# Second pass of the first MoE in chunk pairs: 512 moving columns per weight, one routing per pair

## The chip, the cores and the metric

The kernel runs on one core of a Trainium2 chip. The metric is the device time of one launch in microseconds, as the median of several runs. One of the executions is taken by the hardware profiler; every row below is from that one. PE is TensorE (PEld its weight loads), DVE is VectorE, ACT is ScalarE, POOL is GpSimd, SP is SyncE, which issues most DMAs.

## What is computed

Three stages in a row, cut here to what matters:

```python
attn = softmax(window-128 scores with ALiBi) @ v      # (4, 8, 576, 64)
x = attn as (2304, 512)
h = x @ w_in                                          # (2304, 2048)
x = softplus(h) @ w_out                               # the first MoE, (2304, 512)
logits = x @ w_gate + log1p(exp(x @ w_noise)) * noise # 8 experts
top2 of each token, softmax over the two
out[t] = sum over its two experts of weight * (relu(x[t] @ w1[e]) @ w2[e])
```

## The kernel before, in words

The 2304 tokens go through the first MoE in nine chunks of 256 (`CT`), and the 2048 hidden features in 16 slices of 128 (`NF`). All of a slice of `w_in` and `w_out` is held as a high and a low float32r part. One **unit** is one chunk times one slice: `mm1` (line 574) multiplies the slice of `w_in` with the chunk through `up` (line 539), which is 12 matmuls of 256 moving columns (four pieces of the contraction, three products high-high, high-low, low-high each), into one PSUM bank `h`; then a chain of small operations makes the softplus and splits it into `gh` and `gl` (lines 597 to 606: Abs, Exp and Ln on ACT; `u` and the first sum on DVE; two sums in halves on POOL through `by_halves`, line 570; the cast `gh` and the rest `gl` on DVE); then `mm2` (line 615) multiplies `gh` and `gl` with the slice of `w_out` through `down` (line 563), six matmuls of 512 columns, into the two accumulators of the chunk.

The units stand in the list `jobs` (line 1405). The first pass takes the slices 0 to 5 (`NA`) of all chunks while the attention still runs, and stores partial sums in DRAM. The second pass takes the slices 6 to 15 of chunk 0, then of chunk 1, and so on: 90 units. In the main loop (line 1459) unit t's `mm1` is followed by `mm2` of unit t-3, with `side_work` (line 1425) after each of the two: it takes one step from the list of the routing. `x_load` (line 642) brings a chunk's input back from DRAM for the second pass, `part_load` its partial sum, `y_evac` (line 670) adds the two on DVE and stores the result to `x1buf`.

`route` (line 809) then gives the steps of the router for that chunk: two `r_transpose` (four PE transposes each, ACT copies the result), `r_logits`, `r_sum`, `r_top2` (some 25 small DVE operations), `r_rank` (positions of the tokens in each expert's list, five small matmuls and DVE steps), and then four indirect DMAs on POOL that scatter the records (`rect<-rec,pi`, line 803). `early_table` (line 971) makes from the counts of chunks 0 to 5 the first four groups of the second MoE; their weights (`raw`), record lists (`rk`) and rows (`xg`) are then loaded. In the last seven units of the pass `w2_split` (line 1215) already splits weights of the second MoE, ACT the high part `whi` and DVE the low part `wlo`. The second MoE follows, with `up_wide` (line 555), which already uses 512 columns.

Every engine carries its instructions out in the order in which they were written. That order comes from a planner with modelled costs (`Order`, line 24): a chain's next step is written when the model says that it is due. `tl` gives out tiles in rings: the third tile of a ring of two waits for the first one's last reader.

Of the kernel before, what the change touches and what calls it, by code (L numbers as in the profile page):

```python
# [18 lines left out]
P = 128  # L19
# [91 lines left out]
def moe_chain_kernel(ctx, tc, qk, v, w_in, w_out, w_gate, w_noise, noise, w1, w2, out):  # L111
# [14 lines left out]
    NLEAD = 3  # L126

# [158 lines left out]
    def xt_tile(c):  # L286
        if c not in XT:
            if c == 2:
                XT[c] = tuple(wpool.tile([P, KC, CT], F32R, name=n, tag="w", bufs=NRING) for n in ("xh2", "xl2")) + (None,)
            else:  # L290
                XT[c] = x_tile(2, ("mm1", c))
# [259 lines left out]
    def x_tile(bufs, fin):  # L551
        x2 = tl(mid, [P, 2, KC, CT], F32R, "xhl", bufs, fin)
        return x2[:, 0], x2[:, 1], x2

# [19 lines left out]
    def mm1(t):  # L574
# [10 lines left out]
        if fc == NA:  # L585
            for z in range(2):
                need(("xi", c, z))
            if c + 1 < NCH:
                x_load(c + 1)
        w = W[2 * fc]  # L590
        ph = up(lambda z, kc: w[:, z, kc * P:(kc + 1) * P], XT[c], CT, ("hr", t))
# [23 lines left out]
    def mm2(t):  # L615
        c, fc = divmod(t, NF)
        if c == 0:
            weights(2 * fc + 1)
        need(("g", t))
        gh, gl = G.pop(t)  # L620
        if fc in (0, NA):
            side_by_side = c == 1 and fc == 0
            if side_by_side:
# [18 lines left out]
    def x_load(c):  # L642
        XT[c] = x_tile(2, ("mm1b", c))
        for z, x in enumerate(XT[c][:2]):
            dma(lambda z=z, x=x: SP.dma_start(f32(x).rearrange("p k t -> p (k t)"), xspill[c, z]),
                ("xi", c, z), 1 << 19)
# [17 lines left out]
    def part_load(c):  # L664
        def load():
            x1, flat = x1_tile(c, ("x1", c))
            SP.dma_start(flat, yspill[c])
        dma(load, ("yi", c), 1 << 19)

    def y_evac(c):  # L670
        need(("yi", c))
        x1 = X1[c]
        for a in range(TT):
            chain(("V", cv(512), lambda a=a: DVE.tensor_add(x1[:, a], Y[c][a], x1[:, a]), ("y%d" % a, c)))
        dma(lambda: SP.dma_start(x1buf[c * CT:(c + 1) * CT, :].rearrange("(a p) n -> p a n", p=P), x1),
            ("x1d", c), 1 << 19, 0.7, (("y0", c), ("y1", c)))


    RT = {}

    def r_transpose(c, tt):
        need(("y0", c))
        need(("y1", c))
        pt = ps_t(("x1T", c, tt)).rearrange("p (c t) -> p c t", c=KC)
        for kc in range(KC):
            tr(pt[:, kc, :], X1[c][:, tt, kc * P:(kc + 1) * P], ident)
        if tt == 0:
            RT[c] = tl(mid, [P, KC, CT], F32, "x1T", 1, ("lgm", c))
        else:
            chain((None, 0, None, ("x1", c), (("x1d", c),)))  # L690
        x1T = RT[c][:, :, tt * P:(tt + 1) * P]
        chain(("A", ca(512), lambda: ACT.activation(x1T, pt, AF.Copy), ("x1T", c, tt)))

    def r_logits(c):

        for tt in range(TT):
            need(("x1T", c, tt))
        pl = ps_t(("lgp", c))[:, :CT]
        for kc in range(KC):
            PE.matmul(pl[32 * kc:32 * kc + 32, :], wgn[:, kc, :], RT[c][:, kc, :], start=True, stop=True)  # L700
        spend(4 * CT / 2.4 + 100)
        mark(("lgm", c))
        lgp = RT[c] = tl(mid, [P, CT], F32, "lgp", 1, ("lgs", c))
        chain(("A", ca(CT), lambda: ACT.activation(lgp, pl, AF.Copy), ("lgp", c)))

    def r_sum(c):
        need(("lgp", c))
        pt = ps_t(("lg", c))[:, :CT].rearrange("p (t k) -> p t k", t=TT)
        for tt in range(TT):
            tr(pt[:, tt], RT[c][:, tt * P:(tt + 1) * P], ident)  # L710
        mark(("lgs", c))
        lg = RT[c] = tl(mid, [P, TT, 2 * E], F32, "lg", 1, ("top", c))
        chain(("V", cv(CT), lambda: DVE.tensor_reduce(
# [4 lines left out]
    def small(name, shape, dtype=F32):  # L718
        return mid.tile(shape, dtype, name="r_" + name, tag="r_" + name, bufs=1)

    def r_top2(c):
        lg = RT[c]
        z = lg[:, :, E:]
# [7 lines left out]
        rec = mid.tile([P, TT, 2, 2], I32, name="rec", tag="rec", bufs=2)  # L731
# [11 lines left out]
        step(DVE.tensor_mul, l, l, nz[:, c * TT:(c + 1) * TT, :])  # L743
# [14 lines left out]
        for k2 in range(2):  # L758
            step(DVE.tensor_copy, rec[:, :, k2, 0], tok[:, c * TT:(c + 1) * TT])
# [11 lines left out]
    def r_rank(c):  # L771
        need(("mb", c))
        r = RT[c]
        pr = ps_t(("rk", c))[:, :TT * E].rearrange("p (a e) -> p a e", a=TT)
        if c:
            need(("mc", c - 1))
# [7 lines left out]
        pi = mid.tile([P, 2, TT], I32, name="pi", tag="pi", bufs=2)  # L784
# [16 lines left out]
        for tt in range(TT):  # L801
            for k2 in range(2):
                G_ += [("P", 1.05, lambda tt=tt, k2=k2: POOL.indirect_dma_start(
                    out=rect[2 * tt + k2], out_offset=bass.IndirectOffsetOnAxis(ap=pi[:, k2, tt:tt + 1], axis=0),
# [4 lines left out]
    def route(c):  # L809
        for _ in range(3):  # L810
            yield None
        yield lambda: r_transpose(c, 0)
        yield lambda: r_transpose(c, 1)
# [8 lines left out]
        for _ in range(6 + 2 * (c == NCH - 2) + 3 * (c == NCH - 1)):  # L822
            yield None
# [45 lines left out]
    p2 = None  # L869
# [4 lines left out]
    def open_p2():  # L874
# [4 lines left out]
        p2 = ctx.enter_context(tc.tile_pool(name="p2", bufs=2))  # L879
        for name, n, base, step in (("jm", 2 * NJ, 0, P // 2), ("jpair", NJ // 2, P, 2 * P), ("jfull", NJ // 2, 2 * P, 2 * P),  # L880
# [231 lines left out]
    def g_gather(g):  # L1112
# [3 lines left out]
        for a in range(n):  # L1116
            x = tl(p2, [P, DM], F32, "xg", 6, ("gx", g, a))
# [5 lines left out]
    def g_transpose(g, a):  # L1123
# [5 lines left out]
        if n == 1:  # L1129
            d["xT"] = tl(p2, [P, KC, P], F32, "xs", 2, ("gup", g))  # L1130
            return chain(("A", ca(512), lambda: ACT.activation(d["xT"], pt, AF.Copy), ("gx", g, a)))
        if a == 0:
            d["xT"] = x_tile(2, ("gup", g))
# [40 lines left out]
    def w2_load():  # L1174
# [16 lines left out]
        if more:  # L1191
            extra.add(j)
            t = p2.tile([P, 1024], F32, name="raw2", tag="raw2", bufs=NXTRA)
# [72 lines left out]
    def s1(g, f):  # L1266
# [33 lines left out]
        else:  # L1300
# [13 lines left out]
            hs = tl(p2, [P, 512], F32, "hs", 2, ("ht", g, f))  # L1314
# [5 lines left out]
    def s2(g, f):  # L1320
# [8 lines left out]
        th = tl(p2, [P, 4, P], F32, "th", 2, ("dn", g, f))  # L1329
# [3 lines left out]
    def s3(g, f):  # L1333
# [32 lines left out]
        if f == (NF1 if n == 2 else 2) - 1:  # L1366
            rc = GR[g]["rc"]
            for a in range(n):
                ys = tl(p2, [P, DM], F32, "ys", 4, ("yo", g, a))
# [39 lines left out]
    jobs += [(c, f) for c in range(NCH) for f in range(NA, NF)]  # L1409
# [49 lines left out]
    for t in range(NT + max(L2, len(items) + 3)):  # L1459
# [28 lines left out]
        if t < NT:  # L1488
            c, fc = jobs[t]
            if c == NCH - 1 and fc == 1:  # L1490
                x_load(0)
            mm1(c * NF + fc)
# [15 lines left out]
        if 0 <= t - L2 < NT:  # L1508
# [5 lines left out]
            if fc == NF - 1:  # L1514
                y_evac(c)
                rfeed = chained(rfeed, route(c))
# [68 lines left out]
```

## Time and profile before

| what | value |
|---|---|
| median of three runs | 1075.98 us (1074.99, 1075.98, 1080.08) |
| profiled execution, own time | 1076.8 us |
| its span in the trace | 1075.0 us |
| PE busy | 1029.0 us, 96% of the span |
| DVE, ACT, POOL busy | 751.4, 651.8, 587.9 us |
| mean granted clock of PE | 0.985 |

The profiled execution is 0.8 us above the median and 1.8 us longer than its span. Busy PE counts from a matmul's start to its modelled end, and neighbours overlap; what a matmul costs in a stream is the distance from one start to the next.

### The profile page before, as it was taken

The page shows a single profiled execution, that of the slowest core. Times are in us where ns is not written, and L with a number is a line of the kernel's source. Part 1 is how long each engine was busy: PE and PEld are TensorE (multiplying, and loading weights), DVE is VectorE, ACT ScalarE, POOL GpSimd, SP SyncE. Part 2 cuts the span into 40 slices and gives each one's busy share as a digit, 9 for nine tenths or more (in the row PEclk, how much of TensorE's full clock was granted, in tenths as well). Part 3 has the DMA queues.
Part 4 walks back from the last instruction along what each step waited for, and adds up shares of the span by engine and source line. Part 5 has one row for each costly group of instructions (what it writes and reads, how often), then busy time and mean ns, then how long its engine had stood idle before and what let it go on. Part 6 is the DMA issues. An engine that isn't in the chain of part 4 may idle for free.

```text
span 1075.0 us, 20651 instructions
## 1 busy us (share of the span) xinstructions
PE 1029.0 (96%) x6533; PEld 847.9 (79%) x6533; DVE 751.4 (70%) x2033; ACT 651.8 (61%) x1580; POOL 587.9 (55%) x935
## 2 busy tenths in 40 slices
PE   5699999999999999999999999999999999999995
PEld 3477777777788888898887898888886888688864
DVE  6975787898865556766687678887764776377632
ACT  7976778888764444444446456666654665466641
POOL 4676798989896567777778533321242232133112
PEclk8899999999999999999999999999999999999998
DMA  8331544555684332212236959977789988998642
GB/s 303 128 98 60 191 144 165 192 196 178 191 317 166 97 99 80 79 61 72 67 118 201 371 137 290 269 230 210 204 237 361 308 233 216 334 324 239 193 129 31
DMA packets 97315, 202.07 MB, mean 188 GB/s; under 512 B 34161, under 2 KB 44913, under 8 KB 97201
## 3 DMA queue, kind: packets, MB, share of 16 engines
q1 hardware_dynamic: 87264, 180.21, 50.1%
q0 software_dynamic: 9936, 20.49, 9.6%
q8 instruction: 53, 0.87, 0.3%
q14 instruction: 62, 0.50, 0.2%
HBM read 161.49 MB, written 39.17 MB: 187 GB/s over the span
## 4 chain that ended last, share of the span: by engine, by line
PE 69%; DVE 3%; POOL 3%; DMA 2%; ACT 1%; issue 1%; SPq 0%; POOLq 0%; ACTq 0%; DVEq 0%
PE h L190 31%; PE y L190 20%; PE z L190 10%; PE t L201 3%; PE h L1309 2%; PE y L1359 1%; POOL sl L572 1%; POOL su L572 1%; PE t L190 1%; PE z L1359 1%; DMA rawv<-in_v 1%; PE t L343 1%; DMA out<-ys,rc 1%; DVE wlo L1226 1%; DVE su L605 0%
## 5 line engine op out<-in xcount | busy, mean ns | idle before, releaser
L190 PE MATMUL h<-xhl,w 128*128 128x256 f32 x1656 | 229.3, 288 | 4.3 <-DVE sl L600 3.2
L1372 POOL DMA_INDIRECT out<-ys,rc x42 | 80.9, 1926 | 278.5 <-DVE ys L1382 124.7
L190 PEld LDWEIGHTS h<-xhl,w 128*128 128x128 f32 x1656 | 214.1, 193 | 21.7 <-DVE sl L600 6.4
L190 PE MATMUL h<-xhl,whi 128*128 128x512 f32 (+1 forms) x640 | 210.2, 375 | 0.1
L190 PE MATMUL y<-w,gh 128*128 128x512 f32 x552 | 177.8, 403 | 0.0
L572 POOL TENSOR_TENSOR su<-sa,su 128x128 f32<-128x128 f32 x288 | 137.4, 498 | 70.6 <-DVE su L605 59.7
L1226 DVE TENSOR_TENSOR wlo<-rawp,whi 128x1024 fp32r<-128x1024 f32 x108 | 132.0, 1223 | 48.4 <-ACT whi L1228 37.5
L190 PE MATMUL h<-xhl,wlo 128*128 128x256 f32 x576 | 161.5, 280 | 0.0
L572 POOL TENSOR_TENSOR sl<-sl,su 128x128 f32<-128x128 f32 x288 | 139.8, 506 | 7.2 <-DVE sl L600 5.6
L190 PEld LDWEIGHTS h<-xhl,whi 128*128 128x128 f32 x640 | 116.9, 188 | 29.0 <-issue 3.7
L597 ACT ACTIVATE sa<-h 128x256 f32<-128x256 f32 x144 | 54.8, 381 | 130.9 <-PE h L190 79.1
L1228 ACT ACTIVATE whi<-rawp 128x1024 fp32r<-128x1024 f32 x108 | 113.5, 1055 | 21.0 <-PE h L190 12.3
L190 PEld LDWEIGHTS h<-xhl,wlo 128*128 128x128 f32 x576 | 108.8, 189 | 4.8
L376 POOL TENSOR_TENSOR s<-s,st 128x256 f32<-128x256 f32 (+2 forms) x144 | 92.3, 663 | 29.3 <-DVE st L367 9.6
L190 PE MATMUL y<-w,gl 128*128 128x512 f32 x276 | 108.2, 392 | 0.0
L190 PEld LDWEIGHTS y<-w,gh 128*128 128x128 f32 x552 | 94.2, 189 | 16.0 <-issue 2.4
L1294 ACT ACTIVATE sa<-h 128x256 f32<-128x256 f32 x128 | 48.3, 378 | 94.6 <-PE h L190 93.7
L361 ACT ACTIVATE s<-s,st 128x256 f32<-128x256 f32 (+2 forms) x160 | 76.1, 478 | 17.2 <-DVE st L355 17.1
L604 DVE TENSOR_TENSOR gl<-sl,gh 128x256 fp32r<-128x256 f32 x144 | 69.6, 483 | 20.7 <-ACT gh L602 18.1
L1295 DVE TENSOR_TENSOR sl<-h,sa 128x256 f32<-128x256 f32 x128 | 53.6, 419 | 41.6 <-ACT sa L1294 37.8
L605 DVE TENSOR_SCALAR su<-sa 128x256 f32<-128x256 f32 x144 | 62.0, 430 | 24.9 <-ACT sa L598 23.3
L1118 POOL DMA_INDIRECT xg<-x1buf,rc x39 | 44.5, 1142 | 54.0 <-PE y L190 18.0
(271 smaller groups left out, 2090.1 us busy)
## 6 DMA issues: line engine op xcount, KB each, us to landing
rawp<-in_moe_w SPq DMA_DIRECT2D x144, 512.0 KB
raw<-in_moe_w SPq DMA_DIRECT2D x48, 512.0 KB
qkT<-in_qk SPq DMA_DIRECT2D x20, 512.0 KB
xhl<-xspill SPq DMA_DIRECT2D x18, 512.0 KB
raw<-in_moe_w_in SPq DMA_DIRECT2D x16, 512.0 KB
raw<-in_moe_w_out SPq DMA_DIRECT2D x16, 512.0 KB
xspill<-xhl SPq DMA_DIRECT2D x16, 512.0 KB
out<-zero SPq DMA_DIRECT2D x19, 256.0 KB
```

The source lines that it names most:

```text
L190: PE.matmul(o, l, r, start=start, stop=stop)
L361: ACT.activation(s[:nq, j, :n], s[:nq, j, :n], AF.Exp, bias=st[:nq, 0, y], scale=-1.0, accum_out=sums[:nq, y, 0])
L376: POOL.tensor_tensor(s[:nq, j, :n], s[:nq, j, :n], st[:nq, 3, 2 * x + j:2 * x + j + 1].to_broadcast([nq, n]), OP.mult)
L572: POOL.tensor_tensor(o[:, z], x[:, z], y[:, z], op)
L597: chain(("A", ca(CT), lambda: ACT.activation(a, ph, AF.Abs)), ("A", ca(CT), lambda: ACT.activation(a, a, AF.Exp, scale=-1.0), ("e", t)), ( ...
L604: ("V", cv(CT), lambda: DVE.tensor_sub(gl, l, f32(gh)), ("g", t)))
L605: chain(("V", cv2(CT), lambda: DVE.tensor_scalar(u, a, 1.0, 1.0, op0=OP.add, op1=OP.subtract), None, (("e", t),)), ("P", cg(CT), lambda: b ...
L1226: DVE.tensor_sub(lo, t, f32(hi))
L1228: chain(("A", ca(1024), lambda: ACT.activation(hi, t, AF.Copy), None, (("r2", j),)), ("V", cv(1024), low, ("w2", j)))
L1294: chain(("A", ca(CT), lambda: ACT.activation(b, ph[:, 1], AF.Copy)), ("V", cv(CT), lambda: DVE.tensor_add(s, ph[:, 0], b), ("hr2", g, f)), ...
L1295: ("V", cv(CT), lambda: DVE.tensor_add(s, ph[:, 0], b), ("hr2", g, f)),
L1372: POOL.indirect_dma_start(out=out[:, :], out_offset=bass.IndirectOffsetOnAxis(ap=rc[:sl.stop - sl.start, a + x, 0:1], axis=0), in_=ys[sl], ...
```

## The change

Chunks 0 to 5 go through the second pass in pairs (`NPR = 6`). The job list alternates the two chunks of a pair slice by slice, a new `up_pair` multiplies a weight with both chunks at once into one whole PSUM bank, and each chunk's softplus chain reads its half of the bank. The pair's input stands in one tile: `XX`, the former ring of two, for the pair 2, 3, and a new tile `xxp` for the pairs 0, 1 and 4, 5, in the space that the attention has left. The odd chunk of a pair accumulates in the two `z` tiles of the `t` banks, which leaves two of four to transposes and routing. One routing serves a pair: four transposes, logits of 512 columns, 14 instead of twice 5 rank matmuls, small DVE operations on twice the width, eight scatters with a planned gap of 2 us after the fourth. `open_p2` splits: the first part opens at the end of the first pass, the rest four units later than before, and `early_table` comes three units later.

```diff
+    XX = mid.tile([P, 2, 2, KC, CT], F32R, name="xx", bufs=1)
+    def up_pair(w, xx, fin):
+        ph = tl(psum, [P, 512], F32, "h", 2, fin)
+        i = 0
+        for kc in range(KC):
+            wh, wl = w(0, kc), w(1, kc)
+            for l, z in ((wh, 0), (wh, 1), (wl, 0)):
+                mm(ph.rearrange("p (c t) -> p c t", c=2), l, xx[:, :, z, kc], i == 0, i == 3 * KC - 1)
+                i += 1
+        return ph
...
-        ph = up(lambda z, kc: w[:, z, kc * P:(kc + 1) * P], XT[c], CT, ("hr", t))
+        parts = lambda z, kc: w[:, z, kc * P:(kc + 1) * P]
+        if not pair:
+            ph = up(parts, XT[c], CT, ("hr", t))
+        else:
+            if c % 2 == 0:
+                XW["h"] = up_pair(parts, XW[c], ("hr", t + NF))
+            ph = XW["h"][:, c % 2 * CT:(c % 2 + 1) * CT]
...
-            side_by_side = c == 1 and fc == 0
+            side_by_side = c == 1 and fc == 0 or c < NPR and c % 2 and fc == NA
...
     def route(c):
-        yield lambda: r_transpose(c, 0)
-        yield lambda: r_transpose(c, 1)
+        for tt in range(tiles_of(c)):
+            yield lambda tt=tt: r_transpose(c, tt)
...
-        for _ in range(6 + 2 * (c == NCH - 2) + 3 * (c == NCH - 1)):
+        for _ in range(6 + 2 * (c == NCH - 2) + 3 * (c == NCH - 1) + 3 * (c < NPR) + 2 * (c == NPR)):
             yield None
         yield lambda: r_rank(c)
...
         for tt in range(TT):
+            if tt == 2:
+                G_ += [(None, 2.0, None)]
...
-    jobs += [(c, f) for c in range(NCH) for f in range(NA, NF)]
+    jobs += [(c + i, f) for c in range(0, NPR, 2) for f in range(NA, NF) for i in range(2)]
+    jobs += [(c, f) for c in range(NPR, NCH) for f in range(NA, NF)]
...
-        if t == last_start - (NF - NA):
+        if t == last_start - (NF - NA) + 4:
             open_p2()
-        if t == last_start - (NF - NA) + 3:
+        if t == last_start - (NF - NA) + 6:
             early_table(NCH - 4)
...
             if fc == NF - 1:
                 y_evac(c)
-                rfeed = chained(rfeed, route(c))
+                if c % 2 or c >= NPR:
+                    rfeed = chained(rfeed, route(c))
```

PE in the middle of the second pass, before (`h` is an up product, `y` the down product of the chunk):

```order
L190 MATMUL h<-xhl,w 128x256 x12
L190 MATMUL y<-w,gh 128x512 x2
L190 MATMUL y<-w,gl 128x512
L190 MATMUL y<-w,gh 128x512 x2
L190 MATMUL y<-w,gl 128x512
```

and in the changed kernel (`z` is the down product of the odd chunk):

```order
L191 MATMUL h<-xxp,w 128x512 x12
L191 MATMUL z<-w,gh 128x512 x2
L191 MATMUL z<-w,gl 128x512
L191 MATMUL z<-w,gh 128x512 x2
L191 MATMUL z<-w,gl 128x512
L191 MATMUL y<-w,gh 128x512 x2
L191 MATMUL y<-w,gl 128x512
L191 MATMUL y<-w,gh 128x512 x2
L191 MATMUL y<-w,gl 128x512
```

Two narrow ups have become one wide one; the downs are the same, two now in a row. The `z` is that of two pairs back, the `y` that of one pair back.

POOL at the scatters of the first chunk routed, before (`su` and `sl` with one number are a unit's two sums):

```order
L572 TENSOR_TENSOR sl_5281<-sl_5281,su_5280 128x128 x2
L803 DMA rect0_115<-rec_5159,pi_5310 18688x2
L572 TENSOR_TENSOR su_5334<-sa_5333,su_5334 128x128 x2
L803 DMA rect1_116<-rec_5159,pi_5310 18688x2
L572 TENSOR_TENSOR sl_5335<-sl_5335,su_5334 128x128 x2
L572 TENSOR_TENSOR su_5375<-sa_5374,su_5375 128x128 x2
L803 DMA rect2_117<-rec_5159,pi_5310 18688x2
```

and at those of the first pair in the changed kernel:

```order
L594 TENSOR_TENSOR sl_5547<-sl_5547,su_5546 128x128 x2
L879 DMA rect0_115<-rec_5393,pi_5571 18688x2
L879 DMA rect1_116<-rec_5393,pi_5571 18688x2
L879 DMA rect2_117<-rec_5393,pi_5571 18688x2
L594 TENSOR_TENSOR su_5615<-sa_5614,su_5615 128x128 x2
L879 DMA rect3_118<-rec_5393,pi_5571 18688x2
L594 TENSOR_TENSOR su_5636<-sa_5635,su_5636 128x128 x2
L594 TENSOR_TENSOR sl_5616<-sl_5616,su_5615 128x128 x2
L594 TENSOR_TENSOR sl_5637<-sl_5637,su_5636 128x128 x2
L879 DMA rect0_115<-rec_5393,pi_5571 18688x2
```

Three scatters now stand in a row ahead of the first sum of the next pair, and one more between its sums.

DVE in the last seven units of the pass, where the splits of the second MoE's weights begin; before:

```order
L1226 TENSOR_TENSOR wlo<-raw_7811,whi 128x1024
L603 CAST gh<-sl 128x256
L604 TENSOR_TENSOR gl<-sl,gh 128x256
L605 TENSOR_SCALAR su<-sa 128x256
L600 SCALAR_TENSOR_TENSOR sl<-h,sl 128x256
L1226 TENSOR_TENSOR wlo<-raw_7823,whi 128x1024
```

and in the changed kernel:

```order
L1313 TENSOR_TENSOR wlo<-raw_7438,whi 128x1024
L635 TENSOR_SCALAR su<-sa 128x256
L863 TENSOR_TENSOR r_pp<-r_m_7343,r_rb 128x32
L807 RECIPROCAL r_g<-r_g 128x2
L630 SCALAR_TENSOR_TENSOR sl<-h,sl 128x256
L633 CAST gh<-sl 128x256
L1313 TENSOR_TENSOR wlo<-raw_7450,whi 128x1024
L863 TENSOR_REDUCE r_ps<-r_pp 128x4
L807 COPY rec<-r_g 128x2
L634 TENSOR_TENSOR gl<-sl,gh 128x256
```

The rank of chunk 6 (`r_pp`, `r_ps` and what follows) has moved from ahead of the first split to between the splits.

## Rows read from the trace of the kernel before

**Rows 1.** The page: busy time by engine, and the granted clock in 40 slices.
```profile
PE 1029.0 (96%) x6533; PEld 847.9 (79%) x6533; DVE 751.4 (70%) x2033; ACT 651.8 (61%) x1580; POOL 587.9 (55%) x935
...
PEclk8899999999999999999999999999999999999998
```

**Rows 2.** Busy time of each engine (PE, PEld, DVE, ACT, POOL), granted clock, DMA.
```profile
450.00:500.00 50.00, 50.00 (x339) 44.20 (x338) 32.49 (x117) 23.06 (x61) 35.60 (x74) 1.00 0.22 67
```

**Rows 3.** Timeline of PE, one unit (start us, us, what).
```profile
474.03 1.60 PE L190 MATMUL h<-xhl,w 128*128 128x256 f32 x12
475.46 0.63 PE L190 MATMUL y<-w,gh 128*128 128x512 f32 x2
...
476.85 1.60 PE L190 MATMUL h<-xhl,w 128*128 128x256 f32 x12
```

**Rows 4.** Timeline of PE in the second MoE: 512 and 256 columns in turn.
```profile
860.73 0.39 PE L190 MATMUL h<-xhl,whi 128*128 128x512 f32 x1
860.96 0.28 PE L190 MATMUL h<-xhl,wlo 128*128 128x256 f32 x1
861.07 0.40 PE L190 MATMUL h<-xhl,whi 128*128 128x512 f32 x1
```

**Rows 5.** Timeline of PE: the same unit of two neighbouring chunks.
```profile
468.17 1.59 PE L190 MATMUL h<-xhl,w 128*128 128x256 f32 x12
...
498.47 1.60 PE L190 MATMUL h<-xhl,w 128*128 128x256 f32 x12
```

**Rows 6.** Timeline of PE: a routing transpose, and the logits of one chunk.
```profile
481.11 0.60 PE L201 MATMUL t<-ident,x 128*128 128x128 f32 x4
481.46 0.71 PE L190 MATMUL y<-w,gh 128*128 128x512 f32 x2
...
577.34 0.64 PE L700 MATMUL t<-x1T,wgn 128*32 128x256 f32 x8
577.91 1.70 PE L190 MATMUL h<-xhl,w 128*128 128x256 f32 x12
```

**Rows 7.** Timelines of ACT, DVE and POOL: the chain of one unit.
```profile
478.53 0.38 ACT L597 ACTIVATE sa<-h 128x256 f32<-128x256 f32 x1 [1.53 <-DVE x L674]
...
480.22 0.41 DVE L600 SCALAR_TENSOR_TENSOR sl<-h,sl 128x256 f32<-128x256 f32 x1
...
481.83 0.89 POOL L572 TENSOR_TENSOR su<-sa,su 128x128 f32<-128x128 f32 x2
482.68 0.87 POOL L572 TENSOR_TENSOR sl<-sl,su 128x128 f32<-128x128 f32 x2
...
484.16 0.41 DVE L604 TENSOR_TENSOR gl<-sl,gh 128x256 fp32r<-128x256 f32 x1
```

**Rows 8.** Timeline of POOL: scatters of the first routing.
```profile
384.05 1.15 POOL L803 DMA_INDIRECT rect<-rec,pi  x1 [2.04 <-DVE mcum L789]
...
389.40 0.99 POOL L803 DMA_INDIRECT rect<-rec,pi  x1 [0.16 <-issue]
```

**Rows 9.** Waits, 555 to 605 us (total, times, longest); timeline of DVE there.
```profile
PE h L190 <- DVE sl L600: 2.3, 3, 1.2
...
565.92 0.38 DVE L736 TENSOR_TENSOR rec<-r_g 128x2 f32<-128x2 f32 x1
...
582.37 1.48 DVE L1226 TENSOR_TENSOR wlo<-raw,whi 128x1024 fp32r<-128x1024 f32 x1
```

**Rows 10.** SP issues the first chunk's input; PE starts on it; the stretch between.
```profile
299.44 1.21 SPq L645 DMA_DIRECT2D xhl<-xspill  x2
...
317.99 1.69 PE L190 MATMUL h<-xhl,w 128*128 128x256 f32 x12
...
305.00:310.00 5.00, 5.00 (x34) 4.57 (x33) 3.78 (x7) 3.72 (x10) 5.00 (x9) 1.00 1.04 397
```

**Rows 11.** Timelines of POOL and PE: rows of the first group, gathered and used.
```profile
565.46 0.96 POOL L1118 DMA_INDIRECT xg<-x1buf,rc  x1 [0.30 <-issue]
...
587.67 0.45 PE L201 MATMUL t<-ident_r,xg 128*128 128x128 f32 x4
```

More of the change, by code (lines that the diff above doesn't have):

```diff
@@ L549, in up, with x_tile @@
         return ph
[L551 to L553 removed]
+    XX = mid.tile([P, 2, 2, KC, CT], F32R, name="xx", bufs=1)
+    XW = {}
+    def x_tile(fin):
+        r = rings.setdefault("xx", [])
+        while len(r) >= 2:
+            last = r[-2]
+            emitted(last)
+            if r[-2] == last:
+                break
+        x2 = XX[:, len(r) % 2]
+        r.append(fin)
+        return x2[:, 0], x2[:, 1], x2
+    def up_pair(w, xx, fin):
[7 more added lines that the diff above has]
+        return ph
     def up_wide(w, x2, fin):
@@ L584, in mm1 @@
                     ("xo", c, z), 1 << 19)
[L585 to L589, printed above, removed]
-        w = W[2 * fc]
-        ph = up(lambda z, kc: w[:, z, kc * P:(kc + 1) * P], XT[c], CT, ("hr", t))
+        pair = fc >= NA and c < NPR
+        if fc == NA and not (pair and c % 2):
+            for x in range(c, c + 1 + pair):
+                for z in range(2):
+                    need(("xi", x, z))
+            if c + 1 + pair < NCH:
+                x_load(c + 1 + pair)
+        w = W[2 * fc]
+        parts = lambda z, kc: w[:, z, kc * P:(kc + 1) * P]
[5 more added lines that the diff above has]
+            ph = XW["h"][:, c % 2 * CT:(c % 2 + 1) * CT]
         a = tl(mid, [P, CT], F32, "sa", 2, ("g", t))
@@ L642, in x_load @@
     def x_load(c):
[L643 to L646, printed above, removed]
+        if c < NPR and c % 4 == 0:
+            if c:
+                emitted(("mm1b", c - 3))
+            XW[c] = XW["t"]
+            xs = [(c + i, XW[c][:, i]) for i in range(2)]
+        elif c < NPR:
+            assert len(rings["xx"]) % 2 == 0
+            XW[c] = XX
+            xs = [(c + i, x_tile(("mm1b", c + i))[2]) for i in range(2)]
+        else:
+            XT[c] = x_tile(("mm1b", c))
+            xs = [(c, XT[c][2])]
+        for i, x in xs:
+            for z in range(2):
+                dma(lambda i=i, z=z, x=x: SP.dma_start(f32(x[:, z]).rearrange("p k t -> p (k t)"), xspill[i, z]),
+                    ("xi", i, z), 1 << 19)
     def x1_tile(c, fin):
@@ L664, in part_load, with load @@
     def part_load(c):
+        if c < NPR:
+            for i in range(2):
+                def load(i=i):
+                    if i == 0:
+                        X1["pair"] = tl(XW["pool"], [P, 2 * TT, DM], F32, "x1d", 1, ("x1", c + 1))
+                    X1[c + i] = X1["pair"][:, i * TT:(i + 1) * TT]
+                    SP.dma_start(X1[c + i].rearrange("p a n -> p (a n)"), yspill[c + i])
+                dma(load, ("yi", c + i), 1 << 19)
+            return
         def load():
@@ L758, in r_top2 @@
         for k2 in range(2):
-            step(DVE.tensor_copy, rec[:, :, k2, 0], tok[:, c * TT:(c + 1) * TT])
+            step(DVE.tensor_copy, rec[:, :, k2, 0], tok[:, a0:a0 + TT])
         V.append(("A", 0.2, lambda: ACT.activation(g[:, 1], g[:, 0], AF.Exp)))
@@ L879, in open_p2 @@
         p2 = ctx.enter_context(tc.tile_pool(name="p2", bufs=2))
+        ctx.enter_context(pstack)
+        XW["pool"] = pstack.enter_context(tc.tile_pool(name="pair", bufs=1))
+        XW["t"] = XW["pool"].tile([P, 2, 2, KC, CT], F32R, name="xxp", bufs=1)
+    def open_p2():
+        nonlocal p3
+        for key in ("pi", "mc", "rec"):
+            emitted((key, NPR - 1))
+        pstack.close()
+        p3 = ctx.enter_context(tc.tile_pool(name="p3", bufs=2))
         for name, n, base, step in (("jm", 2 * NJ, 0, P // 2), ("jpair", NJ // 2, P, 2 * P), ("jfull", NJ // 2, 2 * P, 2 * P),
```

94 lines of the change are left out of this document (59 added, 35 removed).

## The prediction

> **What bounds the kernel now.** I read the page first: PE is busy 96% of the span and at its upper clock, 2.4 GHz, in nearly all slices [rows 1]. Then the busy time by stretches: in the second pass PE has no idle time, while POOL has 36 of 50 us of work and DVE 32 [rows 2]. So in this stage time can only come off PE's own stream, and the other engines matter where they make it wait. The timeline of PE gives the price of the stream: an up starts at 474.03, its down at 475.46, the next up at 476.85 [rows 3]. That is 1.43 us for 12 matmuls of 256 columns, 0.119 each, and 1.39 us for six of 512, 0.232 each; a unit is 2.82 us. Last, the waits of PE: none in the middle of the pass, three at its end, 2.3 us together, each for DVE, which is then splitting weights [rows 9]. After it PE does not stop until the tail.
>
> **The change, part by part**, against the profiled execution's own 1076.8 us.
>
> *The wide up.* A pair drops 24 x 0.119 = 2.86 us and adds 12 x 0.232 = 2.78. Where up matmuls already alternate 512 and 256 columns, the distances are 0.23 and 0.11 [rows 4], so neither the strided input nor one bank as target costs extra there. Gain 0.08 us a pair-slice, 30 of them: **-2.4 us**. With the 0.23 and 0.11 of [rows 4] it would be 24 x 0.11 - 12 x 0.23 = -0.12, a loss of 3.6 us in all, which is their rounding to a hundredth; I take the finer figure from the twelve and keep 0 to -2.4 for the range. Half of the weight loads go, but they hide behind the matmuls. The page "TensorE: Matmul & The Clock Gate" of the Trainium skill, section "Wait — 56ns, not 53.3ns?", gives a distance of N / 2.4 plus 2.5 ns, so 109 and 216 ns; by it a pair-slice saves 0.03 us and the whole 0.9 us. The trace is 10 and 16 ns above both, and goes first.
>
> *Routing on PE.* The same unit of two neighbouring chunks stands 30.30 us apart [rows 5]; ten units are 28.2, so one chunk's routing holds PE 2.10 us, two chunks' 4.20. A transpose step is 0.35 us [rows 6] and each break in the stream about 0.1, so four steps in three places cost 1.7, against 1.6 before. Logits take 0.57 for 256 columns [rows 6] plus breaks, 0.85 in all, twice per pair; with 512 columns one step costs between 0.57 and 1.14, say 1.0, and one set of breaks, 1.28: -0.4. One summing step goes (-0.1), and four rank matmuls of 8 columns come, each below the 0.09 of one transposing matmul [rows 6] (+0.1, at most 0.35, and a break goes). Sum 3.8 against 4.2 a pair: **-1.1 us** for three, between -2.5 and +1 (the third transpose now waits for the first one's copy in one of two banks; ACT's copy has 1.7 us for it, up to 0.5 late is possible).
>
> *The softplus chain.* Today a unit's down comes three units after its up: 3 x 1.39 + 3 x 1.43 = 8.46 us after the up's end. In a pair, the first chunk's down follows after z, y, the next wide up and z: 3 x 1.39 + 2.78 = 6.95; the second chunk's after 11.1. The chain needs, for a unit whose up ended at 478.28: Abs 478.53, sum on DVE 480.22, POOL 481.83 to 483.55, rest `gl` finished at 484.57 [rows 7], 6.3 us, 1 us of it a scatter that stood in between. Laid out for a pair with these durations (ACT 1.3 us a chunk, one after the other; POOL 1.8 a chunk), the first `gl` is ready 4.2 us after the up, the second 5.9: in the quiet stretches the margin is 2.7 us and PE does not wait. **0.** PSUM `h` is read out 3.3 us after the up, and the bank is wanted after 8.3.
>
> *Scatters.* A scatter occupies POOL about 1 us, 1.15 with its gap [rows 8]. A pair has eight, over three pair cycles of 5.56 us in which POOL also has 3 x 3.6 us of sums: 9.2 + 10.8 = 20 us in some 19. Three stand in a row ahead of the next pair's first sum. By my layout they push the first `gl` to 6.9 us in that cycle, 6.5 in the next, 7.4 to 7.9 in the third, against 6.95 for `gh` and 7.4 for `gl`. So about 0.5 us of waiting in the third cycle of the first two routings; after the third routing the units are single again, with 8.46 us. **+1.0 us**, from 0 to 7.6 (a rival below).
>
> *The end of the pass.* Here DVE is the limit: a unit's four operations and one `wlo` of 1.48 us [rows 9] are over 2.82 us. The table comes three units later and the rank of chunk 6 with its moves falls between the splits: seven small operations of up to 0.38 us [rows 9], some 2 us, of which DVE's own gaps hide part. **+1.5 us**, from 0 to 3. The rows of the first group were gathered by 566.4 and used at 587.67 [rows 11], 21 us; three units and a little, some 10 us, later is still in time. **0.** If that cover went, PE would stand at the first transposes of the second MoE.
>
> *Loads.* The first pair needs 2 MB instead of 1 MB. SP issued the first chunk at 299.44 and PE started on it at 317.99 [rows 10]. DMA is full then (397 GB/s), so 1 MB more takes some 3 us, of 18. SP's queue behind it holds weights from scratch for slice 9 on, which the alternating order now wants later. **0.** If the loads were late, the first wide up would wait.
>
> Sum: -2.4 - 1.1 + 1.0 + 1.5 = -1.0 us, so 1075.8 on the profiled execution. Its own time is 0.8 above the median of the runs; against the median it is 1075.0. I give **1075.3**, between the two. The second MoE is unchanged and PE never waits in it, so it shifts as a whole.
>
> **The rivals.** A measurement of this kernel can tell about 0.5%, 5.4 us, from no change.
>
> *POOL becomes the bound while it scatters (slower).* A scatter at the head of POOL's queue waits for `rec` and `pi` from DVE, and the sums behind it wait too: at the first routing POOL stood 2.04 us so [rows 8]. Today the 8.46 us swallow that; with 6.95 and three scatters ahead they do not, once the head waits about 1 us. With 2.04 + 0.5 at each of three routings, +7.6, the end at its bound of +3 and the gains of 3.5, it comes to 1083.9, 1083.1 against the median. For it: three scatters in a row. Against: for a pair the last sum of the earlier unit ends after `pi` is made, so POOL should find its data ready. Chance 0.17.
>
> *No new waits.* The scatters fit, the end of the pass costs nothing more or loses one of its three waits: -3.5 - 1.0, so 1072.3, 1071.5 against the median. For it: a pair has fewer DVE steps in routing. Chance 0.15.
>
> *Narrow matmuls are bound by their weights, wide ones are not.* If a wide up went at 0.119 a matmul, a pair-slice would save 1.43 us, 43 us in all: 1034. Against it stands every down, 512 columns at 0.232 [rows 3], and [rows 4]. Chance 0.02. The same page, section "Back-to-back issue gap", states 131 ns for 512 columns in a stream with weight loads; by that the saving would be some 38 us. The trace contradicts the figure.
>
> *It saves nothing at all on PE* (range end 0 of the first term) is inside the forecast: 1077.
>
> **How the numbers follow.** Forecast 0.66, POOL 0.17, no new waits 0.15, weights 0.02. Faster by over 0.5% means below 1070.6: all of the last and a quarter of the third, 0.06. Slower means above 1081.4: 0.6 of the POOL case, 0.10. The same: 0.84. The range runs from 1071 (no new waits) to 1081.5 (into the POOL case, whose upper part, 0.1, is left out with the weights' 0.02 and the lower edge of the third).
>
> **What would show it.** Wide ups should start to end in 2.78 us, pairs follow in 5.56. Right: PE without waits between routings, at most 1 us of waits for `gl` after each pair's scatters, and 3 to 6 us at the end of the pass. Routing of a pair should hold PE 3.8 us: the same unit of two neighbouring pairs 59.4 us apart plus its waits. Wrong: a distance of 512 columns away from 0.232 inside the wide up; POOL idle at a scatter with sums behind it; PE waiting for `xg` or for `xx`.

## The result, and the profile after

| | before | after |
|---|---|---|
| median, us | 1075.82 (6 runs, 1074.86 to 1080.08) | 1086.09 (6 runs, 1085.50 to 1090.15) |
| ratio to before | | 1.0098 (95% interval 1.0087 to 1.0110) |
| profiled execution, own time / span | 1076.8 / 1075.0 | 1085.6 / 1083.6 |
| mean granted clock of PE | 0.985 | 0.984 |

The changed kernel is 10.3 us slower; the forecast was 1075.3 with a range up to 1081.5. So the prediction was wrong. The page of the changed kernel (busy time by engine) hardly shows it:

```profile
PE 1026.0 (95%) x6161; PEld 830.6 (77%) x6161; DVE 754.3 (70%) x1967; ACT 647.0 (60%) x1565; POOL 587.1 (54%) x935
```

PE has 3 us less work than before [rows 1] and a span 8.6 us longer. To find the stage, I read PE's timeline at the borders: the second pass begins, the first unit of chunk 6 begins, the second MoE begins. Before, these stand at 317.99, 498.47 [rows 5, 10] and 593.30. After:

```profile
316.30 3.00 PE L191 MATMUL h<-xxp,w 128*128 128x512 f32 x12
...
494.61 1.59 PE L191 MATMUL h<-xx,w 128*128 128x256 f32 x12
...
601.31 0.28 PE L191 MATMUL h<-xx,whi 128*128 128x256 f32 x1
```

The paired chunks 0 to 5 take 178.3 us, 2.2 less than before (180.5). Chunks 6 to 8, which the change leaves single, take 106.7 against 94.8: **11.9 us more**. What comes behind differs by 0.6, and the start by 1.7 (it lies between 316.0 and 319.4 in all runs below, without any order in it). The loss is where nothing was paired.

The pairs first, on PE's timeline: a wide up, and the logits of a pair.

```profile
321.92 2.93 PE L191 MATMUL h<-xxp,w 128*128 128x512 f32 x12
324.68 0.63 PE L191 MATMUL y<-w,gh 128*128 128x512 f32 x2
...
395.29 1.06 PE L762 MATMUL t<-x1Td,wgn 128*32 128x512 f32 x8
396.29 0.73 PE L191 MATMUL y<-w,gh 128*128 128x512 f32 x2
```

From start to start 2.76 and 1.00 us. Now PE at the end of the pass, with the idle time before an instruction and what ended it in brackets:

```profile
585.88 1.67 PE L191 MATMUL h<-xx,w 128*128 128x256 f32 x12
587.38 0.46 PE L202 MATMUL t<-ident_r,xg 128*128 128x128 f32 x4
594.14 1.22 PE L191 MATMUL y<-w,gh 128*128 128x512 f32 x2 [6.31 <-ACT gh L632]
598.02 1.70 PE L191 MATMUL h<-xx,w 128*128 128x256 f32 x12 [0.95 <-DVE sl L630]
```

One wait of 6.31 us for `gh`, made on ACT from POOL's sums. It is most of what the view of PE's waits lists from 490 to 640 us (total, times, longest); of these, 10.1 us lie ahead of the second MoE (all but the wait for `xx`), where before there were 2.3 [rows 9]:

```profile
PE y L191 <- ACT gh L632: 6.3, 1, 6.3
PE h L191 <- DVE sl L630: 3.0, 3, 1.5
PE h L191 <- DVE xx L1224: 0.7, 1, 0.7
PE y L191 <- DVE x L726: 0.5, 1, 0.5
PE y L191 <- DVE gh L633: 0.3, 1, 0.3
```
POOL's timeline in the same stretch:

```profile
581.68 1.61 POOL L1205 DMA_INDIRECT xg<-x1buf,rc  x1 [0.30 <-issue]
589.70 0.99 POOL L879 DMA_INDIRECT rect<-rec,pi  x1 [6.41 <-DMA rk<-rect]
590.73 0.86 POOL L594 TENSOR_TENSOR su<-sa,su 128x128 f32<-128x128 f32 x2
```

POOL stood still for 6.41 us at the first scatter of chunk 6, with the softplus sums queued behind it. Its own data had long been there (DVE's timeline):

```profile
578.06 0.38 DVE L863 CAST pi<-r_ps 128x4 int32<-128x4 f32 x1
578.35 0.15 DVE L807 TENSOR_TENSOR rec<-r_g 128x2 f32<-128x2 f32 x1
```

It waited for DMAs that **read** the buffer that the scatter writes. SP issues them among the weight loads of the second MoE (timeline of SP):

```profile
576.87 1.79 SPq L1177 DMA_DIRECT2D rk<-rect  x1
...
583.32 0.37 SPq L1177 DMA_DIRECT2D rk<-rect  x1
583.94 0.37 SPq L1285 DMA_DIRECT2D rawp<-in_moe_w  x1
```

`rect` is four copies of the record buffer, scattered into by two tiles and two ranks. The first groups of the second MoE read their record lists from all four as soon as the early table is known; chunk 6 writes into the same copies later. Whichever is written first in the program, the other waits for it. Before, chunk 6's four scatters started at 567.49 to 576.59, ahead of all but two of the reads of the second and later groups. After, its routing comes later, and the first scatter stands behind the second group's reads and one read of the third. That one was issued at 583.32, and these reads took this long from issue to landing (the view of tile `rk`, 570 to 600 us):

```profile
DMA to landing us min/median/max: 4.7/5.4/6.0
```

583.32 and 6 us give 589.3; the scatter went at 589.70.

A last part is the clock (columns: PE, PEld, DVE, ACT, POOL busy, PE's granted clock, DMA share, GB/s):

```profile
585.00:590.00 5.00, 2.84 (x22) 2.48 (x21) 0.00 (x0) 0.00 (x0) 0.30 (x1) 1.00 1.04 380
590.00:595.00 5.00, 0.86 (x2) 0.71 (x3) 0.82 (x2) 0.71 (x3) 4.61 (x9) 0.58 0.90 325
595.00:600.00 5.00, 4.05 (x22) 3.07 (x22) 4.36 (x10) 3.33 (x12) 4.38 (x8) 0.74 0.62 42
```

During the wait PE's clock fell to its lower level, 1.2 GHz, and stayed there for a few microseconds of work: the two matmuls at 594.14 take 1.22 us, where 0.63 is usual (at 324.68).

### The profile page after: what moved, and what is told of

It reads as the page before. It is cut to its first block, busy times and chain, and to the rows that moved or that the text cites. A ratio compares the mean times of both kernels' runs of the same rounds, so it can differ in the third digit from the quotient of the medians.

```text
span 1083.6 us, 19825 instructions
## 1 busy us (share of the span) xinstructions
PE 1026.0 (95%) x6161; PEld 830.6 (77%) x6161; DVE 754.3 (70%) x1967; ACT 647.0 (60%) x1565; POOL 587.1 (54%) x935
## 4 chain that ended last, share of the span: by engine, by line
PE 61%; POOL 7%; DVE 6%; issue 2%; ACT 2%; DMA 1%; SPq 0%; POOLq 0%; DVEq 0%; ACTq 0%
PE h L191 27%; PE y L191 14%; PE z L191 12%; POOL sl L594 3%; PE t L202 3%; PE h L1396 2%; POOL su L594 2%; POOL rect L879 2%; PE y L1446 1%; DVE su L635 1%; PE t L191 1%; DVE gl L634 1%; PE z L1446 1%; PE t L344 1%; DVE sl L630 1%
## 5 line engine op out<-in xcount | busy, mean ns | idle before, releaser
L191 PE MATMUL h<-xx,whi 128*128 128x512 f32 (+1 forms) x640 | 210.2, 375 | 0.7 <-DVE xx L1224 0.7
L191 PE MATMUL h<-xx,w 128*128 128x256 f32 (+1 forms) x1056 | 160.6, 303 | 4.8 <-DVE sl L630 3.8
L191 PE MATMUL h<-xx,wlo 128*128 128x256 f32 x576 | 161.8, 281 | 0.0
L191 PEld LDWEIGHTS h<-xx,w 128*128 128x128 f32 x1056 | 143.5, 193 | 21.0 <-DVE sl L630 7.5
L191 PE MATMUL y<-w,gh 128*128 128x512 f32 x432 | 141.4, 409 | 10.7 <-ACT gh L632 6.3
L191 PEld LDWEIGHTS h<-xx,whi 128*128 128x128 f32 x640 | 117.0, 188 | 29.6 <-issue 2.4
L627 ACT ACTIVATE sa<-h 128x256 f32<-128x256 f32 x144 | 54.4, 378 | 142.2 <-PE h L191 102.1
L191 PEld LDWEIGHTS h<-xx,wlo 128*128 128x128 f32 x576 | 109.0, 189 | 4.7
L191 PEld LDWEIGHTS y<-w,gh 128*128 128x128 f32 x432 | 75.5, 190 | 30.1 <-ACT gh L632 6.4
L634 DVE TENSOR_TENSOR gl<-sl,gh 128x256 fp32r<-128x256 f32 x144 | 74.7, 519 | 30.5 <-ACT gh L632 27.6
L191 PE MATMUL y<-w,gl 128*128 128x512 f32 x216 | 85.7, 397 | 0.0
```

The costliest lines, as they stand in the source:

```text
L191: PE.matmul(o, l, r, start=start, stop=stop)
L627: chain(("A", ca(CT), lambda: ACT.activation(a, ph, AF.Abs)), ("A", ca(CT), lambda: ACT.activation(a, a, AF.Exp, scale=-1.0), ("e", t)), ( ...
L634: ("V", cv(CT), lambda: DVE.tensor_sub(gl, l, f32(gh)), ("g", t)))
```

## The experiments

Every ratio is against the kernel before, run on the same chip. The theories at the start: **A**, the order of chunk 6's scatters and the record reads is the loss; **B**, POOL and DVE have too much to do since the routing comes in pairs, whatever the order; **C**, the pairs themselves (late sums, scatters) cost it. After the first four runs a theory **D** was added. The stages of all runs are from PE's timeline of each profiled execution (chunks 0 to 5: start of the pass to chunk 6's first unit; chunks 6 to 8: from there to the first matmul of the second MoE; rest: to the end of the span). That one execution can lie some us off the median (e2 3.1, e11 2.6, e7 1.9 and e9 1.7 us below it), so the stages say where time went, and the medians and ratios how much:

| run | median us | ratio, 95% interval | chunks 0-5 | chunks 6-8 | rest |
|---|---|---|---|---|---|
| before | 1075.8 to 1077.2 | | 180.5 | 94.8 | 481.7 |
| after | 1086.1 | 1.0098 (1.0087-1.0110) | 178.3 | 106.7 | 482.3 |
| e1_rank6_early | 1086.3 | 1.0080 (1.0062-1.0099) | 178.4 | 105.0 | 481.3 |
| e2_reads_held | 1091.6 | 1.0136 (1.0114-1.0158) | 178.3 | 103.0 | 488.8 |
| e3_before_rank6_late | 1084.0 | 1.0054 (1.0034-1.0074) | 180.5 | 99.3 | 483.2 |
| e4_pair_narrow | 1091.3 | 1.0120 (1.0099-1.0142) | 180.5 | 109.3 | 481.1 |
| e5_two_pairs | 1078.2 | 1.0010 (0.9996-1.0023) | 180.5 | 96.1 | 481.8 |
| e6_tail_early | 1094.5 | 1.0169 (1.0149-1.0188) | 178.3 | 115.1 | 481.3 |
| e7_tail_early_held | 1088.8 | 1.0119 (1.0097-1.0141) | 178.3 | 102.1 | 488.7 |
| e8_spread | 1084.7 | 1.0074 (1.0055-1.0092) | 174.3 | 103.5 | 486.5 |
| e9_all | 1078.8 | 1.0023 (1.0013-1.0032) | 174.3 | 101.0 | 483.3 |
| e10_two_pairs_spread | **1074.5** | **0.9975** (0.9965-0.9985) | 178.8 | 94.9 | 482.0 |
| e11_reads_held2 | 1085.9 | 1.0090 (1.0074-1.0105) | 178.4 | 103.0 | 482.4 |
| e12_table_split | 1080.1 | 1.0030 (1.0018-1.0042) | 178.4 | 100.0 | 482.0 |

**The loss put into the kernel before** (e3). In `route` of the kernel before; each round of this loop holds the routing back by one call of `side_work`, a half step:

```diff
-        for _ in range(6 + 2 * (c == NCH - 2) + 3 * (c == NCH - 1)):
+        for _ in range(6 + 2 * (c == NCH - 2) + 3 * (c == NCH - 1) + 5 * (c == 6)):
```

> The kernel before (1075.8 us), unpaired, with one edit: the rank of chunk 6 five slots later, so that its scatters are issued behind six record reads, as in the changed kernel. Theory A: the loss appears in a kernel that has no pair in it: POOL's first scatter of chunk 6 waits 4 to 7 us for record reads, TensorE waits for the sums behind it, and the time is 1080 to 1085 us. Rival B (the pairs cost it): under 1 us, 1075 to 1077 us.

1084.0 against 1077.2, 6.7 us slower by the medians and inside what A expected. POOL's and PE's timelines of this run, the last two lines the borders of chunks 6 to 8:

```profile
586.66 1.00 POOL L803 DMA_INDIRECT rect<-rec,pi  x1 [6.84 <-DMA rk<-rect]
...
591.12 1.22 PE L190 MATMUL y<-w,gh 128*128 128x512 f32 x2 [4.00 <-ACT gh L602]
...
499.84 1.60 PE L190 MATMUL h<-xhl,w 128*128 128x256 f32 x12
...
599.16 0.39 PE L190 MATMUL h<-xhl,whi 128*128 128x256 f32 x1 [0.68 <-DVE r_l L736]
```

As A had it: a kernel without one pair shows the same wait of POOL (6.84 against 6.41), once chunk 6's scatters stand behind reads. It does not show the whole price: chunks 6 to 8 take 99.3 us here, 4.5 more than before, against 11.9 more in the changed kernel. Of the rest of this execution's loss, 1.5 us lie behind the pass and 1.4 in its later start.

**The wide up priced by itself** (e4). `up_pair` as two narrow ups in the halves of its bank:

```diff
-            for l, z in ((wh, 0), (wh, 1), (wl, 0)):
-                mm(ph.rearrange("p (c t) -> p c t", c=2), l, xx[:, :, z, kc], i == 0, i == 3 * KC - 1)
...
+                for l, z in ((wh, 0), (wh, 1), (wl, 0)):
+                    mm(ph[:, c * CT:(c + 1) * CT], l, xx[:, c, z, kc], i == 0, i == 3 * KC - 1)
```

> The changed kernel with the pair's up done as two narrow ones of 256 columns, one behind the other, in the two halves of the same bank; all else stays, the routing in pairs too. Theory A (the wide up is a gain of its own, about 0.08 us per pair and slice, and no part of the loss): 2 to 3 us slower than the changed kernel, 1088 to 1089 us. Rival C (the wide up delivers both chunks' sums late and is what makes TensorE wait): the same or faster than the changed kernel, 1080 to 1086 us.

1091.3, above the 1088 to 1089 expected, though by the ratios (1.0120 and 1.0098) it is some 2.4 us slower than the changed kernel. In chunks 0 to 5 it is 2.2 us slower (180.5 against 178.3): the wide up is a gain of about the predicted 2.4 us and no part of the loss; C falls for the ups. The other 2.6 us lie in chunks 6 to 8, which this edit does not touch; that stretch moves by microseconds with any shift of the order, and I read no price from it here.

**Chunk 6's rank earlier, alone** (e1).

```diff
-        for _ in range(6 + 2 * (c == NCH - 2) + 3 * (c == NCH - 1) + 3 * (c < NPR) + 2 * (c == NPR)):
+        for _ in range(6 + 2 * (c == NCH - 2) + 3 * (c == NCH - 1) + 3 * (c < NPR) - 2 * (c == NPR)):
```

> The changed kernel (1086.1 us), with the rank of chunk 6 four slots earlier, so that its four scatters are issued in the order of the kernel before, ahead of most of the record reads of the second group of experts. Theory A (the 8 us wait of TensorE at 586 to 598 us is chunk 6's first scatter standing behind record reads on the same buffer): the wait is gone, the first matmul of the second MoE comes at about 593 us and the time is 1077 to 1079 us. Rival B (POOL and VectorE simply have too much to do since the routing comes in pairs, whatever the order): the wait moves but keeps its size, 1084 to 1087 us.

1086.3: a miss for A as put. POOL's wait for reads is gone, but PE's timeline has a new one:

```profile
569.41 0.19 PE L191 MATMUL t<-r_mb,tri 128*128 128x8 bf16 x1 [5.99 <-DVE r_mb L807]
```

PE stood 5.99 us at chunk 6's rank matmul, since DVE had not yet found the top two. DVE was behind: the early table, emitted three units later in the change, ran until 570.0 in this run, right through chunk 6's routing; in the kernel before it was done at 551.9, just ahead of it (552.4). So the last pair's long routing pushes the early table, and with it chunk 6, into one heap; this is read from the timelines. That is **theory D**: the crowd at the end of the pass is what makes chunk 6 late, and the record reads multiply what lateness costs.

**The reads held back, alone** (e2, then e11). Reads past the first group wait until chunk 6's last scatter is issued (`free`); the edit also plans the merge of the second group's records 7 us after its reads instead of 14:

```diff
-        read_rows()
+        for _ in range(2 if free else 1):
+            if reads and (reads[0][0] == 0 or free):
+                read_rows()
```

> The changed kernel with chunk 6 routed where the change routes it, but the record reads of every group past the first held back until chunk 6's last scatter is issued, then two at a time. Theory A: the scatter waits for no read, TensorE's wait at 586 to 598 us falls from 8 us to under 2, and the time is 1077 to 1081 us (a little of it may come back later, since the second group's rows are gathered some 8 us later than in the changed kernel). Rival B (the lateness of chunk 6's routing itself, or the load on POOL and VectorE): 1084 to 1087 us.

The wait of 6.3 us fell to 1.2 and the second MoE began 3.4 us earlier, yet the total was 1091.6: a miss, with 6.5 us lost behind the pass. My edit issued two reads per load to the end of the program, and DVE's merges then stood in its queue waiting for records (5.9 us at 600 to 720 us), and PE for DVE's sums behind them (6.3 us in three, the longest 3.2). The same with the double reading limited to the first four groups:

> The changed kernel with the record reads held as in the earlier try, but two at a time only up to the fourth group, one at a time after. The earlier try reached the second MoE at 597.9 us, 3.4 us ahead of the changed kernel, and lost 6.5 us behind it; if that loss is the later groups' records read too early (VectorE's merges then wait for them), the time is now 1082 to 1084 us. If holding the reads back is itself the loss, 1088 us or more.

1085.9: the rest is back at 482.4, but the time is above the 1082 to 1084 expected, and level with the changed kernel. Chunks 6 to 8 stay at 103.0, 3.7 better than after but 8.2 worse than before, and PE waits there in pieces of up to 2.0 us, mostly for DVE. So the order of the reads is not the whole loss when chunk 6 is late anyway, and taking it away by itself gave nothing that the medians show.

**The end of the pass earlier** (e6). The last pair's rank one half step, the early table one unit, and chunk 6's rank three half steps earlier:

```diff
-        for _ in range(6 + 2 * (c == NCH - 2) + 3 * (c == NCH - 1) + 3 * (c < NPR) + 2 * (c == NPR)):
+        for _ in range(6 + 2 * (c == NCH - 2) + 3 * (c == NCH - 1) + 3 * (c < NPR) - (c == NPR - 1)):
...
-        if t == last_start - (NF - NA) + 6:
+        if t == last_start - (NF - NA) + 5:
             early_table(NCH - 4)
```

> The changed kernel with three pairs, the end of the pass earlier: the last pair's rank one half step, the early table one step and chunk 6's rank three half steps in all ahead of where the change has them; record reads where they were, so that three of chunk 6's scatters stand among reads of the second group. Theory D: VectorE reaches chunk 6's top two about 4 us earlier, so that neither the rank nor POOL waits longer than 2 to 4 us; 1079 to 1082 us. Theory A alone (the reads ahead of the scatters are all that counts): the scatters still stand behind reads, 1083 to 1086 us.

1094.5, slower than either theory said. PE waited 11.35 us in one piece. POOL's scatters and SP's reads of this run show why:

```profile
579.92 0.98 POOL L879 DMA_INDIRECT rect<-rec,pi  x1 [4.96 <-DMA rk<-rect]
...
586.91 1.40 POOL L879 DMA_INDIRECT rect<-rec,pi  x1 [0.30 <-issue]
...
597.12 1.00 POOL L879 DMA_INDIRECT rect<-rec,pi  x1 [7.10 <-DMA rk<-rect]
```

```profile
585.28 0.37 SPq L1177 DMA_DIRECT2D rk<-rect  x1
...
592.00 0.37 SPq L1177 DMA_DIRECT2D rk<-rect  x1
...
593.16 0.37 SPq L1177 DMA_DIRECT2D rk<-rect  x1
```

The earlier scatters had come between the reads, and now the two queues wait for each other in turn: a scatter for a read (4.96), SP's next reads for the scatters (it issues at 585.28 and 592.00, nothing between but one weight load), the last scatter for a read behind those (7.10). Interleaved was worse here than behind.

The same kernel with the reads held (e7; the second group's merge is planned 10 us after its reads instead of 14):

> As the kernel with the earlier end of the pass, and the record reads past the first group held back until chunk 6's last scatter is issued, then two at a time. Theory D with A (both the crowd on VectorE and the reads ahead of the scatters): no wait of TensorE over 3 us at the end of the pass, 1076 to 1079 us. Theory D alone: within 1 us of the kernel without the holding back.

Chunks 6 to 8 fall from 115.1 to 102.1 us by the hold and what comes with it, which is A's strongest number. One wait of 3.3 us is left there, and the total, 1088.8, missed for the reason already told (rest 488.7). And the same kernel without the hold, but with the order repaired at its source, by taking small operations off DVE ahead of chunk 6 (e12):

```diff
+        chain(*tb.steps)
+        tb.steps = []
         early, upto = TB["early_of"], TB["early_upto"] = tb.row("of", [E]), tb.row("up", [E])
...
-        chain(*tb.steps)
+        chain(*tb.steps, after=40.0)
```

> The kernel with the earlier end of the pass (1094.5 us, where chunk 6's last scatter was issued behind the second group's and two of the third group's reads), with one edit: the second half of the early table is put off by 40 us. That takes about ten small operations from VectorE's queue ahead of chunk 6's top two, and so all four scatters are issued in the order of the kernel before, with one read among them. No read is held. Theory D with A: POOL waits no more than 1 to 2 us for reads, TensorE's 11 us wait is gone and the clock does not fall; 1080 to 1084 us (the first pairs' scatters are not spread here, 4 us). If it is the mere number of operations on POOL and VectorE, the 10 operations give back no more than their own 2 to 3 us: 1091 to 1093 us.

1080.1 against 1094.5 (ratios 1.0030 and 1.0169): 14.4 us from moving eight small operations, which take 1.9 us together on DVE's timeline of the run with the rank earlier. POOL's scatters are now unhindered:

```profile
570.87 1.03 POOL L879 DMA_INDIRECT rect<-rec,pi  x1 [0.16 <-DVE mcum L863]
...
576.33 1.02 POOL L879 DMA_INDIRECT rect<-rec,pi  x1 [0.17 <-issue]
```

That is D with A: the operations' own 1.9 us can't be it; the scatters now go before the reads. They also start 9 us earlier (570.87 against 579.92), and this run does not part the two.

**The first pairs' scatters spread** (e8). On top of the kernel with the earlier end and the reads held, one scatter per half step instead of three in a row:

```diff
+                if c < NPR - 1:
+                    G_ += [(None, 1.6, None)]
```

> As the kernel before this one (end of the pass earlier, reads held), and the scatters of the first two pairs no longer three in a row: one by one, a half step apart. If the waits for gh at 372 to 450 us (2.8 us in three, the longest 1.5) come from three scatters ahead of a chunk's sums on POOL, they fall under 1 us and the time by 1 to 2 us. If they come from VectorE's top two in that stretch, nothing changes.

Chunks 0 to 5 fall from 178.3 to 174.3 us and the waits for `gh` from 2.8 us to none; the median falls by about 4, more than expected. The scatters cost their pairs 4.0 us; so much of C holds. All mends together (e9):

> Three pairs with all mends together: scatters of the first two pairs spread, the end of the pass earlier, the second half of the early table (which only the late table needs) 40 us later, and the record reads held until chunk 6's last scatter is issued, then two at a time for the groups up to the fourth and one at a time after them. Theory D with A: no wait of TensorE over 3 us before the second MoE and none at 650 to 700 us, first matmul of the second MoE at 593 to 595 us, 1075 to 1079 us. If the pairs have a price of their own beyond these waits: 1081 us or more.

1078.8, as expected: 1.8 us above the kernel before on the same chip (1077.0), where the changed kernel was 10.3 above. The clock does not fall any more, and no wait is over 1.5 us (PE, 490 to 640 us, the first three lines):

```profile
PE h L191 <- DVE sl L630: 3.1, 5, 1.1
PE h L191 <- DVE xx L1231: 1.4, 1, 1.4
PE t L191 <- DVE r_mb L807: 0.9, 1, 0.9
```

Still, chunks 6 to 8 take 101.0 us, 6.2 more than before. Some 2 us of it is, by estimate from a pair's routing, work that moved: chunk 4's routing was done before chunk 6 began, now it comes with its pair. Waits like these, 5.2 us in place of 2.3, are 2.9 more; some 1.3 us are not accounted for. Against the run with the table split, which has neither the spread nor the hold, all mends together gain only 1.3 us by the medians, though chunks 0 to 5 are 4.1 shorter; why the later stages give most of it back no run shows.

**Two pairs instead of three** (e5; `NPR = 4`, chunks 4 and 5 single in the space of `xxp`, tables timed as before):

> The changed kernel with two pairs in place of three: chunks 0 to 3 in pairs, chunks 4 to 8 one by one, and the early table and the end of the pass timed as in the kernel before. Theory D (what costs is that the last pair's routing, twice as long and three half steps longer, runs into the early table and chunk 6's routing, so that VectorE, POOL and the record reads all come due at once): no wait over 3 us at the end of the pass, 1074 to 1076 us, two thirds of the gain of the wide ups (1.6 us) less the waits for scatters. Rival C (the pairs themselves, their scatters or the rows that wait for them, cost the time wherever they stand): 1079 to 1084 us.

1078.2, level with before within the interval (ratio 0.9996 to 1.0023), though above the 1074 to 1076 expected; the end of the pass is back at 96.1 us. The pairs' gain is eaten by their scatters: waits for `gh`, 1.9 us, longest 1.5. With these spread (e10):

> The kernel with two pairs, and its pairs' scatters spread one by one. If the three in a row are what cost 1.9 us there (waits for gh, longest 1.5), the time falls by 1.5 to 2 us to 1075 to 1076 us, level with the kernel before or up to 1.5 us faster. If not, it stays within 0.5 us of the kernel with two pairs.

**1074.5, faster than both kernels** and a little below the 1075 to 1076 expected: 0.9975 of the kernel before (0.9965 to 0.9985), 2.5 us. Chunks 0 to 5 are 1.7 us shorter than without the spread, about what the waits were. What waits are left at the end of the pass (PE, 495 to 650 us) is one line, as before [rows 9]:

```profile
PE h L191 <- DVE sl L630: 2.4, 3, 0.9
```

## Why the prediction was wrong

*The wide up, -2.4:* right. 2.76 us against 2.78, cycles of 5.44 to 5.54 us against 5.56, and 2.2 us between narrow and wide ups. The distance of 512 columns inside a wide up is 2.76 / 12 = 0.230. The 131 ns that the Trainium skill states ("TensorE: Matmul & The Clock Gate", section "Back-to-back issue gap") is again not what this stream shows.

*Routing on PE, -1.1:* nearly right per pair. Logits took 1.00 us as assumed; a pair's routing stretched four cycles of 5.44 to 7.15, 6.77, 5.91 and 5.90, together 3.97 us against 3.8. Not seen: the third pair's routing lies wholly behind the pairs, so half of it, some 2 us, moves into the end of the pass, where DVE and POOL are full.

*The softplus chain, 0:* right; in cycles without scatters PE does not wait.

*Scatters, +1.0:* the mechanism was right, the size was off. The three cycles with waits are 7.36, 6.43 and 6.77 us long against 5.44 to 5.53, by difference to the spread kernel's cycles 1.92 + 0.90 + 1.24 = 4.06 us. The layout gave half a microsecond in one cycle for each routing. Its own count pointed higher: it set POOL's 20 us against "some 19", but three cycles of 5.56 us are 16.7.

*The end of the pass, +1.5 (0 to 3):* **this step failed.** It counted DVE's splits and small operations, and the rows of the first group ("21 us" of cover). That cover shrank to 4.1 us (583.29 to 587.38) and still held. What it left out is the other DMA of that stage: the record reads, which share a buffer with chunk 6's scatters. The stage cost 11.9 us: waits of PE of 10.1 us in place of 2.3, some 2 us of routing moved in, and some 2 us more, about what the lower clock explains by estimate: 0.86 us of work before 595, and 2.6 us behind it by the 0.74 of that row, at half speed instead of full, cost 1.7. The change moved chunk 6's scatters past a queue, SP's, and I had followed POOL and DVE, not SP.

The reads are a part of the miss and not all of it. Put into the kernel before they cost the stage 4.5 us; taken out of the changed kernel they gave the stage 3.7 back and the median nothing. With the scatters ahead of the reads again and the table split, the stage is still 5.2 us above before. So the +1.5 for DVE was too small as well: that the last pair's routing, the early table and chunk 6's routing now fall together costs several us more, and went only in the runs where the last chunks stay single (96.1 and 94.9 us).

*The POOL rival* came close in price (1083.1) and had the right form, a scatter at the head of POOL's queue with sums behind it. Its place and its cause were wrong: it stood at the pairs' routings and waited for DVE; in the trace the scatter at the head was chunk 6's, and it waited for reads. That its price came close is luck. The signs named as wrong ("POOL idle at a scatter with sums behind it") were the ones that appeared.

What stays open: the 4 us between the mended three pairs (1078.8) and the two pairs (1074.5) are put down to moved routing work and small waits by the traces alone; no run separates them. Nor does any run part chunk 6's lateness from the crowd on DVE that makes it late.

## What to carry to other kernels

Where a change delays a step, list every buffer that the step writes and ask who reads that buffer on other queues at that time: an order that nobody wrote down (most scatters, then the reads) was worth 4 us or so of the stage, more than the whole gain, and was lost by 12 us of delay (chunk 6's `rec` was done at 566.3 before and at 578.5 after). Two queues that alternated on one buffer were worse here than either order, and a hold, or a few small operations taken off the path to the first writer, repaired that. Pair what is far from the end of a stage, and leave the last items single, so that their long tail does not meet the next stage's start.

## What the runs showed of the hardware

A read of 2 KB took 4.7 to 6.0 us from issue to landing while 512 KB weight loads were under way, and the POOL engine itself stood until it had landed. The Trainium skill ("DMA: Bandwidth & Descriptors", section "Anatomy of one DMA — SWDGE (gpsimd) path") says that a wait for a semaphore is done by the issuing sequencer and not by the DMA engines; that agrees with POOL's 6.41 us. The fixed cost of about 2 us in that section of the Trainium skill, fitted on the path of GpSimd, is under half of what these reads took, which SP issued.

PE's granted clock fell, in 5 us stretches, in each of the five runs with one wait of 4.0 us or more at the end of the pass: to 0.58 in the changed kernel (6.31 us), 0.66 with the rank earlier (5.99), 0.50 in the kernel before with the late rank (4.00) and with the narrow ups (6.3), and to 0.50 to 0.60 over 15 us in the run with the 11.35 us wait:

```profile
590.00:595.00 5.00, 0.00 (x0) 0.00 (x0) 0.00 (x0) 1.43 (x3) 0.03 (x1) 0.60 0.37 115
595.00:600.00 5.00, 0.37 (x1) 0.37 (x2) 0.92 (x2) 0.08 (x1) 2.73 (x5) 0.50 0.89 315
600.00:605.00 5.00, 5.00 (x21) 4.42 (x21) 4.34 (x11) 1.99 (x8) 4.12 (x7) 0.54 0.83 252
```

In the last row PE is busy throughout at about half its clock, so a long wait is paid for a second time behind it. Shorter waits gave no clear line. After one of 3.3 us it fell in one run (0.82) and not in another; in both it fell in the second MoE (to 0.66 and 0.77), after waits of 2.96 and 2.93 us, while after one of 3.22 in the first run with the reads held it did not. In the two runs whose only mend was the held reads it fell (to 0.72 and 0.66) after waits of 1.1 and 2.0 us that stood close together. With waits of at most 1.5 us, in the kernels with the table split, all mends or two pairs, it did not fall there.
